# Attention blocks and MLP on one core: a list-scheduled instruction order, K halves by DMA, Q casts on GpSimd, and block 1's loads ahead of the weights

## The chip, the cores and the metric

One core of one Trainium2 chip. The metric is the device time of one execution in microseconds (us). The kernel before takes 338.56 us (median of three runs, 338.56 to 338.8). A profiled run also has a "span", from its first to its last instruction; it is about 2 us shorter than that run's device time. The profile of before was taken of a run of 340.03 us.

Engines in the profile: PE is TensorE's matmuls, PEld its weight loads, DVE is VectorE, ACT is ScalarE, POOL is GpSimd, SP is SyncE. A "q" behind the name (SPq, ACTq, POOLq) is the engine's sequencer issuing DMAs.

## The reference, cut to what matters

```python
batch, n_heads, seq, head_dim = (4, 8, 768, 64)        # q, k, v, float32
n_tokens, d_model, d_ff = (3072, 512, 2048)            # w_in, w_out, float32
def _attn_ref(q, k, v):                                # chunk = 32, top_k = 6
    ub = np.sum(np.maximum(q[..., None, :] * k_min, q[..., None, :] * k_max), axis=-1)  # bound per query and key chunk
    ...                                                # causal; the 6 chunks with the highest bound are kept
    scores = np.where(mask, scale * np.matmul(q, k.transpose(0, 1, 3, 2)), -1000000000.0)
    ...                                                # softmax
    return np.matmul(attn, v)
def _moe_ref(x, w_in, w_out):                          # x: the heads side by side, 3072 x 512
    h = x @ w_in
    g = np.where(h > 0.0, h, np.exp(np.minimum(h, 0.0)) - 1.0)
    return g @ w_out
```

## The kernel before

The work is cut into eight blocks: four batches, each in two halves of 384 queries. A block has four pairs of heads. Per pair there is a **front** (turn K and Q on TensorE, copy them, compute the bounds, select chunks), an **attention** part (scores, exp, mask, times V, normalize to `on`), and a transpose of `on` to `xt`: on TensorE in blocks 0 and 7, by a DMA on SyncE's queue in the others. When all four `xt` of a block are there, its **MLP** runs: 64 matmuls 128x384 into `h_ps` (called h below), exp, ELU to `gT`, 48 matmuls 128x512 into `o_ps` (called o), store. The next block's front and attention overlap with it.

The parts that the change touches (cuts are marked with `...`):

```python
def prep(t, hf):                                     # front of one pair
    ...
    for n in range(3):
        nc.tensor.transpose(ps[:, P * n:P * (n + 1)], k_pair[:, n], ident_f)   # psK
    ...                                              # VectorE: chunk minima and maxima, kmm and kst
    for h in range(2):                               # ScalarE: K of each head to lhs
        nc.scalar.activation(out=lhs[s][h][0:64, ts], in_=ps[64 * h:64 * h + 64, :], func=AF.Copy)
    ...                                              # psQ, the same way
    nc.scalar.activation(out=QTf[:, q0:HS], in_=ps[:, q0:HS], func=AF.Copy)
    for h in range(2):                               # ScalarE: Q of each head to rhs
        nc.scalar.activation(out=rhs[s][h][0:64, ts], in_=ps[64 * h:64 * h + 64, :], func=AF.Copy)
...
for t in pairs_of(0):
    load_v(t, 0)
front(0, span(-1, 0.0, 0.9))
casts = vpart(0)
w_ins = []
with tc.issue_after(casts[1].ins):                   # the weights, as soon as block 0's V is cast
    w_ins += [load_w_in(0), load_w_in(1)]
with tc.issue_after(casts[3].ins):
    w_ins += [load_w_in(2), load_w_in(3)]
    for i in range(4):
        load_w_out(i)
for i in range(len(blocks)):
    ...                                              # attend(...) x4, then mlp(...)
    if i + 1 < len(blocks):
        for d in load_block(i + 1):
            if i == 0:                               # block 1's loads wait for the whole w_in
                tc.add_manual_dep(d.ins, w_ins[GATE].ins.name, SYNC, reason="order")
        if i == 0:
            with tc.issue_after(mm_h[HGATE].ins):    # block 1's front after block 0's sixth h tile
                front(i + 1, at)
        ...
```

Each instruction has a priority from its stage (`span`, `at`), and the framework's scheduler orders each engine by it.

The softmax here doesn't subtract the row's maximum and nothing guards it: scores larger than these inputs give would overflow.

Of the kernel before, what the change touches and what calls it, by code (L numbers as in the profile page):

```python
# [9 lines left out]
AOT = mybir.AluOpType  # L10
# [5 lines left out]
B = 4  # L16
# [19 lines left out]
PE_T = (0, 7)  # L36
GATE = 3
HGATE = 5
SP_A = [(0.0, 0.5)] + [(0.0, 0.9)] * 7
SP_F = [(0.5, 1.0)] + [(0.0, 0.8)] * 7  # L40
SP_M = [(0.0, 1.0)] * 8
# [3 lines left out]
QHI = (HS, S)  # L45


@with_exitstack
def kernel(
# [9 lines left out]
    nc = tc.nc  # L59

    def pool(name, bufs, **kw):
        return ctx.enter_context(tc.tile_pool(name=name, bufs=bufs, **kw))

    const = pool("const", 1)
    ldpool = pool("ldpool", 4)
    qfpool = pool("qfpool", 3)
    smpool = pool("smpool", 4)
    selpool = pool("selpool", 3)
    ptpool = pool("ptpool", 9)
    opool = pool("opool", 3)  # L70
    xtpool = pool("xtpool", 12)
    gtpool = pool("gtpool", 2)
    mlppool = pool("mlppool", 4)
    psT = pool("psT", 1, space=bass.MemoryType.PSUM)
    psS = pool("psS", 2, space=bass.MemoryType.PSUM)
    psO = pool("psO", 1, space=bass.MemoryType.PSUM)
    psM = pool("psM", 4, space=bass.MemoryType.PSUM)

    warm = const.tile([P, 1], F32, name="warm")
    nc.vector.memset(warm, 0.0)  # L80
    nc.scalar.activation(out=warm, in_=warm, func=AF.Exp)
# [4 lines left out]
    def load_one(dst, x, t, hf, name, eng=nc.sync):  # L86
        b, r = divmod(t, NPAIR)
        xp = ldpool.tile([P, 3, 2, D], F32, name=name)
        dst[t, hf] = xp
        return [eng.dma_start(out=xp[:, :, h, :],  # L90
                              in_=x[b, 2 * r + h, HS * hf:HS * (hf + 1)].rearrange("(n p) d -> p n d", p=P))
                for h in range(2)]

    def load_qk(t, hf):
        first = t < 2 and hf == 0
        return (load_one(ldk, k, t, hf, "k_pair")
                + load_one(ldq, q, t, hf, "q_pair", nc.scalar if first else nc.sync))

    def load_v(t, hf):
        return load_one(ldv, v, t, hf, "v_pair")  # L100

    for t in range(NPAIR):
        load_qk(t, 0)


    ident_f = const.tile([P, P], F32, name="ident_f")
    nc.gpsimd.memset(ident_f, 0.0)
    nc.gpsimd.affine_select(out=ident_f, in_=ident_f, compare_op=AOT.not_equal,
                            fill=1.0, base=0, pattern=[[-1, P]], channel_multiplier=1)


    vexts, lhs, rhs, kst = [], [], [], []
    for s in range(NSET):
        vexts.append(const.tile([P, NQT, 2, D + 1], BF16, name=f"vext{s}"))
        lhs.append([const.tile([P, S], BF16, name=f"lhs{s}{h}") for h in range(2)])
        rhs.append([const.tile([P, S], BF16, name=f"rhs{s}{h}") for h in range(2)])
        kst.append(const.tile([P, 2, 2, CHUNK], F32, name=f"kst{s}"))

    eone = const.tile([P, NCH, 1], BF16, name="eone")
    nc.gpsimd.memset(eone, MASKNEG)  # L120
    nc.gpsimd.affine_select(out=eone[64:96], in_=eone[64:96],
                            compare_op=AOT.is_equal, fill=0.0, base=0,
                            pattern=[[1, NCH], [0, 1]], channel_multiplier=-1)
    econst = const.tile([P, NCH, CHUNK], BF16, name="econst")

    def init_set(s):
        for h in range(2):
            nc.vector.tensor_copy(out=lhs[s][h][64:96, :],
                                  in_=econst[64:96].rearrange("p c w -> p (c w)"))
            nc.gpsimd.memset(rhs[s][h][64:96, 0:Q0], 0.0)  # L130
        nc.gpsimd.memset(vexts[s][:, :, :, D:D + 1], 1.0)

    hsel = const.tile([P, 2], F32, name="hsel")
    for h in range(2):
        nc.gpsimd.memset(hsel[64 * h:64 * h + 64, h:h + 1], 1.0)
        nc.gpsimd.memset(hsel[64 * (1 - h):64 * (1 - h) + 64, h:h + 1], 0.0)
    for s in range(NSET):
        nc.gpsimd.memset(kst[s], 0.0)  # L138

    ident_b = const.tile([P, P], BF16, name="ident_b")  # L140
    nc.gpsimd.tensor_copy(out=ident_b, in_=ident_f)
    tri01 = const.tile([P, P], BF16, name="tri01")
    nc.gpsimd.memset(tri01, 1.0)
    nc.gpsimd.affine_select(out=tri01, in_=tri01, compare_op=AOT.is_ge,
                            fill=0.0, base=0, pattern=[[1, P]], channel_multiplier=-1)
    selb = []
    for hf in range(2):
        nb = (QHI[hf] - QLO[hf]) // CHUNK
        selb.append([const.tile([P, nb, CHUNK], BF16, name=f"selb{hf}{i}") for i in range(2)])
        for i in range(2):  # L150
            nc.gpsimd.memset(selb[hf][i], 0.0)

    w_in_sb = const.tile([P, NKK, DFF], BF16, name="w_in_sb")
    w_out_sb = const.tile([P, NFC, DMODEL], BF16, name="w_out_sb")
# [3 lines left out]
    def load_w_in(i):  # L158
        return nc.gpsimd.dma_start(out=w_in_sb[:, :, 512 * i:512 * (i + 1)], in_=wi[:, :, 512 * i:512 * (i + 1)])

    def load_w_out(i):
        nc.gpsimd.dma_start(out=w_out_sb[:, 4 * i:4 * i + 4, :], in_=wo[:, 4 * i:4 * i + 4, :])

    def cast_v(t, hf):
        return nc.gpsimd.tensor_scalar(out=vexts[t % NSET][:, 3 * hf:3 * hf + 3, :, 0:D], in0=ldv.pop((t, hf)),
                                       scalar1=1.0, scalar2=0.0, op0=AOT.mult, op1=AOT.add)
# [4 lines left out]
    def prep(t, hf):  # L171
        s = t % NSET
        ts = slice(HS * hf, HS * (hf + 1))
        k_pair, q_pair = ldk.pop((t, hf)), ldq.pop((t, hf))
        kmm = smpool.tile([P, 2, HCH], F32, name="kmm")
        pool0 = (psM, "psm") if (t < NPAIR and hf == 0) else (psT, "ps")
        ps = pool0[0].tile([P, HS], F32, name="psK", tag=pool0[1])
        for n in range(3):
            nc.tensor.transpose(ps[:, P * n:P * (n + 1)], k_pair[:, n], ident_f)  # L179
        pv = ps[:, :].rearrange("p (c w) -> p c w", w=CHUNK)  # L180
        nc.vector.tensor_reduce(out=kmm[:, 0, :], in_=pv, axis=AX.X, op=AOT.min)  # L181
        nc.vector.tensor_reduce(out=kmm[:, 1, :], in_=pv, axis=AX.X, op=AOT.max)  # L182
        for h in range(2):
            nc.scalar.activation(out=lhs[s][h][0:64, ts], in_=ps[64 * h:64 * h + 64, :], func=AF.Copy)  # L184
        cs = slice(HCH * hf, HCH * (hf + 1))
        nc.vector.tensor_tensor(out=kmm[:, 1, :], in0=kmm[:, 1, :], in1=kmm[:, 0, :], op=AOT.subtract)
        nc.vector.tensor_tensor(out=kst[s][:, :, :, cs],
                                in0=kmm[:, :, :].rearrange("p (w o) c -> p w o c", o=1)
                                .to_broadcast([P, 2, 2, HCH]),
                                in1=hsel[:, :].rearrange("p (o h u) -> p o h u", o=1, u=1)  # L190
                                .to_broadcast([P, 2, 2, HCH]), op=AOT.mult)
        q0 = QLO[hf] - HS * hf
        QTf = qfpool.tile([P, HS], F32, name="QTf")
        Qrl = qfpool.tile([P, HS], F32, name="Qrl")
        qf[t, hf] = (QTf, Qrl)
        ps = pool0[0].tile([P, HS], F32, name="psQ", tag=pool0[1])
        for n in range(3):
            nc.tensor.transpose(ps[:, P * n:P * (n + 1)], q_pair[:, n], ident_f)  # L198
        nc.scalar.activation(out=QTf[:, q0:HS], in_=ps[:, q0:HS], func=AF.Copy)  # L199
        for h in range(2):  # L200
            nc.scalar.activation(out=rhs[s][h][0:64, ts], in_=ps[64 * h:64 * h + 64, :], func=AF.Copy)
        nc.vector.tensor_scalar(out=Qrl[:, q0:HS], in0=QTf[:, q0:HS], scalar1=0.0, scalar2=None,  # L202
                                op0=AOT.max)


    def select(g, hf):
        qlo, qhi = QLO[hf], QHI[hf]
        nq = qhi - qlo
        nb = nq // CHUNK
        b0 = qlo // CHUNK  # L210
        ncs = qhi // CHUNK
        q0 = qlo - HS * hf
        pool0 = (psM, "psm") if (g < 2 and hf == 0) else (psT, "ps")
        ub = pool0[0].tile([P, HS], F32, name="ub", tag=pool0[1])
        for w in range(2):
# [8 lines left out]
        if b0 + 1 < 8:  # L224
            nc.vector.memset(ubT[:, 0, b0 + 1:8], -BIG)
        thr8 = selpool.tile([P, HCH, 8], F32, name="thr8")
        for i in range(nb):
            nc.vector.max(out=thr8[:, i, :], in_=ubT[:, i, 0:max(8, b0 + i + 1)])
# [222 lines left out]
```

## Time and profile before

| | before |
|---|---|
| device time, median of 3 | 338.56 us |
| span of the profiled run (of 340.03 us) | 338.3 us |
| TensorE / VectorE / ScalarE / GpSimd busy | 90 / 66 / 68 / 29 % |
| first h matmul / last o_sb copy | 32.6 / 335.4 us |

From the page of the kernel before: busy us with share of the span and number of instructions; then the busy tenths of TensorE in 40 slices of 8.5 us (PEclk is the granted TensorE clock in tenths); then the chain of waits that ended last, by engine.

```profile
span 338.3 us, 6875 instructions
PE 303.8 (90%) x2328; PEld 165.8 (49%) x2328; DVE 223.2 (66%) x690; ACT 231.4 (68%) x506; POOL 98.3 (29%) x219
...
PE   3776999998899979999989998999999998999895
...
PEclk9955799999999998999999999999999999999999
...
PE 32%; DVE 24%; issue 18%; ACT 17%; POOL 5%; DMA 3%; SPq 0%; POOLq 0%; ACTq 0%
```

TensorE looks full, and yet the chain that decides the time runs over TensorE for only 32% of the span. The page "Perfetto Trace Analysis" of the Trainium skill (section "Identifying the Most-Contended Engine") says that the matmul busy share is not a good measure of how close TensorE is to its peak.

So I use another measure throughout, worked out from the traces. At full clock the matmuls of one kind start 162 ns (h), 216 ns (o), 30 ns (times V) and 109 ns (fp32 transposes) after one another. Giving each matmul its own full-clock time of this kind, all 2,328 add up to 262.5 us of **matmul work** (an estimate: what one gives the small kinds that are not listed here shifts the sum and the waits below by up to 1.5 us, in all kernels alike). Where a matmul starts later than the one before it allows, that is TensorE's **wait**. Before, from the first matmul at 4.1 us: 36.5 us of waits for matmuls that start in the first 100 us, 32.4 us after that.

What TensorE waited for, from the view of waits (engine, line, tile, what released it: us in total, times, longest us). It lists only gaps that the trace can attribute. The 4.1 us of the second line are the wait from the span's start; the first K load landed at 4.0 us.

```profile
PE h_ps L321 <- DMA xt<-on: 4.6, 5, 2.3
PE psK L179 <- POOL kst_146 L138: 4.1, 1, 4.1
PE pxt L306 <- DVE on L299: 3.7, 3, 1.4
PE h_ps L321 <- DVE gT L328: 3.5, 8, 1.0
```

Busy time of each engine in four stretches (from:to in us, length, then busy us and number of instructions of each engine, mean granted clock, DMA share, GB/s):

```profile
0.00:32.00 32.00, 20.27 (x137) 12.34 (x137) 25.06 (x82) 16.58 (x34) 18.80 (x63) 0.77 0.99 181
32.00:60.00 28.00, 26.49 (x146) 13.61 (x147) 19.56 (x56) 17.63 (x39) 9.99 (x20) 0.90 0.87 180
60.00:100.00 40.00, 35.95 (x323) 19.73 (x321) 28.46 (x100) 36.25 (x80) 4.97 (x10) 1.00 0.40 98
100.00:320.00 220.00, 206.41 (x1653) 113.06 (x1652) 144.94 (x445) 155.37 (x343) 60.19 (x119) 0.99 0.30 76
```

Two things to read here. In the first 32 us VectorE (third count) is busy 25.06 us and ScalarE (fourth) 16.58 us. And after 100 us no engine but TensorE comes near its limit: ScalarE has 155 of 220 us. The DMA share (the time of the packets over that of 16 engines), on the other hand, is 0.99 in the first stretch and 0.87 in the second.

The operations that the change takes from ScalarE, from the list of groups (columns: line, engine, operation, tiles, shapes, count, busy us, mean ns). There are 32 such groups of four, two shown; per pair and half the kernel makes two `lhs` and two `rhs` copies of 0.49 us.

```profile
L184 ACT ACTIVATE lhs_143<-psK 64x384 bf16<-64x384 f32 x4 | 1.9, 487 | 0.0
L201 ACT ACTIVATE rhs_139<-psQ 64x384 bf16<-64x384 f32 x4 | 1.9, 487 | 0.0
```

The end of the start phase, from the timeline of TensorE (start us, duration, engine, line, operation, shapes, count, and in brackets the idle time before it):

```profile
32.27 0.50 PE L306 MATMUL pxt<-ident_b,on 128*128 128x128 bf16 x3 [1.36 <-DVE on L299]
32.56 6.50 PE L321 MATMUL h_ps<-xt,w_in_sb 128*128 128x384 bf16 x24
```

The first h waits for the last pair's `on` and not for the weights: `w_in` had landed by 26.5 us.

### The profile page before, as it was taken

To read this page: it belongs to the slowest core of one execution; us is meant where nothing else is said; L and a number is where in the kernel's file an instruction comes from. 1 tells how busy PE (TensorE), PEld (TensorE's weight loads), DVE (VectorE), ACT (ScalarE), POOL (GpSimd) and SP (SyncE) were. 2 spreads that over 40 slices of the span, in tenths; PEclk is the share of its full clock that TensorE was granted. 3 is DMA by queue.
4 is the path that set the end of the run, shared out by engine and by line. 5 is a ranking of instruction groups with operands and counts; after the bars stand their busy time and mean duration, and the time that the engine had idled before them with its cause. 6 is when DMAs were issued, how large, how long until landed. Compare 5 with 4: busy or idle time off the path is not lost.

```text
span 338.3 us, 6875 instructions
## 1 busy us (share of the span) xinstructions
PE 303.8 (90%) x2328; PEld 165.8 (49%) x2328; DVE 223.2 (66%) x690; ACT 231.4 (68%) x506; POOL 98.3 (29%) x219
## 2 busy tenths in 40 slices
PE   3776999998899979999989998999999998999895
PEld 2444544444454435555654455555554445545552
DVE  5888578566798673875479874866479765622640
ACT  5643585799995718976797649966797647856531
POOL 8750442000055214641153003420053004400530
PEclk9955799999999998999999999999999999999999
DMA  7899977542422677566232313223200111000001
GB/s 175 163 186 202 200 161 175 155 114 60 103 51 60 137 179 186 133 140 148 71 87 52 98 56 89 61 58 92 75 14 12 45 39 37 0 33 34 31 24 69
DMA packets 94498, 32.16 MB, mean 95 GB/s; under 512 B 87296, under 2 KB 91392, under 8 KB 94464
## 3 DMA queue, kind: packets, MB, share of 16 engines
q1 hardware_dynamic: 88640, 27.15, 32.8%
q0 software_dynamic: 4224, 4.19, 7.6%
q10 hardware_dynamic: 1600, 0.39, 0.5%
q8 instruction: 18, 0.29, 0.4%
q14 instruction: 16, 0.13, 0.1%
HBM read 27.26 MB, written 6.29 MB: 99 GB/s over the span
## 4 chain that ended last, share of the span: by engine, by line
PE 32%; DVE 24%; issue 18%; ACT 17%; POOL 5%; DMA 3%; SPq 0%; POOLq 0%; ACTq 0%
PE o_ps L334 11%; PE h_ps L321 9%; DVE gT L328 6%; ACT pt L265 5%; ACT e_sb L325 4%; PE sps L262 4%; PE ub L220 3%; POOL e_sb L326 3%; DMA xt<-on 2%; DVE kmm L181 2%; DVE kmm L182 2%; PE psK L179 1%; DVE on L299 1%; DVE ubT L223 1%; DMA v_pair<-in_v_dram 1%
## 5 line engine op out<-in xcount | busy, mean ns | idle before, releaser
L326 POOL TENSOR_SCALAR e_sb<-e_sb 128x384 f32<-128x384 f32 x128 | 65.7, 521 | 190.8 <-ACT e_sb L325 186.9
L321 PE MATMUL h_ps<-xt,w_in_sb 128*128 128x384 bf16 x512 | 107.1, 334 | 8.3 <-DMA xt<-on 4.6
L334 PE MATMUL o_ps<-w_out_sb,gT 128*128 128x512 bf16 x384 | 99.5, 379 | 0.9 <-DVE gT L328 0.8
L328 DVE SCALAR_TENSOR_TENSOR gT<-h_ps,e_sb 128x384 bf16<-128x384 f32 x128 | 69.1, 552 | 32.7 <-POOL e_sb L326 30.9
L265 ACT ACTIVATE pt<-sps 128x384 bf16<-128x384 f32 (+1 forms) x160 | 79.0, 538 | 16.6 <-PE sps L262 15.3
L325 ACT ACTIVATE e_sb<-h_ps 128x384 f32<-128x384 f32 x128 | 61.3, 502 | 30.5 <-PE h_ps L321 29.9
L321 PEld LDWEIGHTS <-w_in_sb 128*128 128x128 bf16 x512 | 49.6, 100 | 40.8 <-issue 17.2
L334 PEld LDWEIGHTS <-gT 128*128 128x128 bf16 x384 | 35.4, 97 | 36.5 <-issue 3.8
L337 ACT ACTIVATE o_sb<-o_ps 128x512 f32<-128x512 f32 x24 | 14.3, 598 | 35.4 <-PE o_ps L334 32.2
L293 PEld LDWEIGHTS <-pt 128*128 128x128 bf16 x672 | 29.2, 100 | 17.6 <-DVE pt L274 5.1
L274 DVE TENSOR_TENSOR pt<-pt,tri_196 128x512 bf16<-128x512 bf16 x32 | 14.3, 446 | 18.8 <-ACT pt L265 18.8
L179 PE MATMUL psK<-ident_f,k_pair 128*128 128x128 f32 x96 | 20.0, 300 | 6.1 <-POOL kst_146 L138 4.1
L181 DVE TENSOR_REDUCE kmm<-psK 128x12 f32<-128x384 f32 x32 | 17.6, 550 | 6.3 <-PE psK L179 6.1
L268 ACT ACTIVATE pt<-sps 128x512 bf16<-128x512 f32 x32 | 19.5, 609 | 2.6 <-PE sps L262 2.2
L199 ACT ACTIVATE QTf<-psQ 128x192 f32<-128x192 f32 (+1 forms) x32 | 13.2, 413 | 10.1 <-PE psQ L198 7.0
L198 PE MATMUL psQ<-ident_f,q_pair 128*128 128x128 f32 x96 | 18.3, 304 | 1.2 <-ACT lhs_155 L184 0.3
L202 DVE TENSOR_SCALAR Qrl<-QTf 128x192 f32<-128x192 f32 (+1 forms) x32 | 11.7, 365 | 11.5 <-ACT QTf L199 11.0
L179 PEld LDWEIGHTS psK<-ident_f,k_pair 128*128 128x128 f32 x96 | 12.0, 149 | 13.0 <-POOL kst_146 L138 4.1
L182 DVE TENSOR_REDUCE kmm<-psK 128x12 f32<-128x384 f32 x32 | 17.5, 547 | 0.0
L198 PEld LDWEIGHTS psQ<-ident_f,q_pair 128*128 128x128 f32 x96 | 11.3, 151 | 11.8 <-ACT lhs_155 L184 2.0
L280 DVE TENSOR_TENSOR pt<-pt,tri_196 128x256 bf16<-128x256 bf16 x32 | 10.6, 333 | 7.7 <-ACT pt L268 7.7
L223 DVE STREAM_TRANSPOSE ubT<-ub 128x192 f32<-128x192 f32 (+1 forms) x16 | 7.7, 480 | 11.3 <-PE ub L220 11.3
(348 smaller groups left out, 400.7 us busy)
## 6 DMA issues: line engine op xcount, KB each, us to landing
k_pair<-in_k_dram SPq DMA_DIRECT2D x64, 96.0 KB, 2.5
v_pair<-in_v_dram SPq DMA_DIRECT2D x64, 96.0 KB, 2.4
out_dram<-o_sb SPq DMA_DIRECT2D x24, 256.0 KB, 2.1
q_pair<-in_q_dram SPq DMA_DIRECT2D x60, 96.0 KB, 2.4
w_in_sb<-in_moe_w_in_dram POOLq DMA_DIRECT2D x4, 512.0 KB, 8.4
w_out_sb<-in_moe_w_out_dram POOLq DMA_DIRECT2D x4, 512.0 KB, 17.0
q_pair<-in_q_dram ACTq DMA_DIRECT2D x4, 96.0 KB, 2.9
xt<-on SPq DMA_TRANSPOSE x24, 2.4
```

Source lines behind the costliest of these rows:

```text
L179: nc.tensor.transpose(ps[:, P * n:P * (n + 1)], k_pair[:, n], ident_f)
L181: nc.vector.tensor_reduce(out=kmm[:, 0, :], in_=pv, axis=AX.X, op=AOT.min)
L182: nc.vector.tensor_reduce(out=kmm[:, 1, :], in_=pv, axis=AX.X, op=AOT.max)
L198: nc.tensor.transpose(ps[:, P * n:P * (n + 1)], q_pair[:, n], ident_f)
L265: nc.scalar.activation(out=pt[:, hd, 0:wtot], in_=sps[:, 0:wtot], func=AF.Exp, scale=SCALE)
L268: nc.scalar.activation(out=pt[:, :, 0:256], in_=sps[:, :].rearrange("p (h w) -> p h w", h=2), func=AF.Exp, scale=SCALE)
L293: nc.tensor.matmul(o3[:, hd, qi, :], lhsT=pt[:, hd, P * qt + off:P * qt + off + P], rhs=vexts[s][:, kb, hd, :], start=(kb == 0), stop=(kb ...
L321: mm = nc.tensor.matmul(hw, lhsT=w_in_sb[:, kk, P * fc:P * (fc + 1)], rhs=xT[NPAIR * b + kk, hf], start=(kk == 0), stop=(kk == NKK - 1))
L325: nc.scalar.activation(out=e_sb, in_=hw, func=AF.Exp)
L326: last_e = nc.gpsimd.tensor_scalar(out=e_sb, in0=e_sb, scalar1=-1.0, scalar2=1.0, op0=AOT.add, op1=AOT.mult)
L328: nc.vector.scalar_tensor_tensor(out=gT[:, fc, :], in0=hw, scalar=0.0, in1=e_sb, op0=AOT.max, op1=AOT.min)
L334: nc.tensor.matmul(o_ps, lhsT=gT[:, fc, P * tt:P * (tt + 1)], rhs=w_out_sb[:, fc, :], start=(fc == 0), stop=(fc == NFC - 1))
```

## The change

Its intent has four parts. (1) **Order**: the kernel no longer leaves the order to the framework. It states every operation with its engine, its duration and its latency, list-schedules them itself, and emits the instructions in that order. (2) **K and Q**: from block 2 on, K is cast once on ScalarE (`kb`) and its two halves moved to `lhs` by DMAs on SyncE's queue; Q's halves are cast by GpSimd from `QTf`. (3) **Start**: block 1's loads and front come before the weights' DMAs. (4) Fronts may run further ahead, as far as buffers allow. The arithmetic is the same.

```diff
 def prep(...):
-        for h in range(2):
-            nc.scalar.activation(out=lhs[s][h][0:64, ts], in_=ps[64 * h:64 * h + 64, :], func=AF.Copy)
+        if direct:                                   # i in DIRECT = (0, 1); as before
...
+        else:
+            kb = buf("kb", [P, HS], BF16)
+            op("ACT", 390, 140, lambda: nc.scalar.activation(out=kb.get(), in_=psk.get(), func=AF.Copy),
+               reads=[psk], writes=[kb])
+            for h in range(2):
+                op("SP", 490, (200, ), lambda h=h: nc.sync.dma_start(
+                    out=lhs[s][0:64, h, ts], in_=kb.get()[64 * h:64 * h + 64]), reads=[kb], writes=[r_lhs[s][hf]])
...
+            for h in range(2):
+                pool_op(480, lambda h=h: nc.gpsimd.tensor_scalar(
+                    out=rhs[hf][g][0:64, h, j, :], in0=qtf.get()[64 * h:64 * h + 64], scalar1=1.0, scalar2=0.0,
+                    op0=AOT.mult, op1=AOT.add), [r_q[hf][g][j]], [qtf])
...
+    def run(self):                                   # class Plan: greedy list schedule
...
+                    t = max(o.ready, free[e])        # earliest start: inputs, engine, a free buffer
+                    for x in o.bufs:
+                        if x not in held:
+                            t = max(t, min(slots[x.cls], default=1e18))
+                    if t < 1e17 and (best[e] is None or (t, o.prio, o.id) < best[e][:3]):
+                        best[e] = (t, o.prio, o.id, o)
...
+    loads(0)
+    front(0)
+    loads(1)
...
+    casts = front(1)
+    span(-0.2, 0.0, 0.1)
+    for i in range(4):
+        load_w_in(i, [casts[0]])                     # after block 1's first V cast
+    for i in range(4):
+        load_w_out(i, [casts[0]])
...
+    plan.run()
+    with tc.manual_schedule():
+        for o in plan.order:
+            o.fn()
```

The other lines of the diff mostly rewrite every `nc.engine.op(...)` as `op(engine, duration, latency, ...)`. Two things go with it: `rhs` and `selb` are laid out in other buffers, and the Q loads of the first two pairs are issued by SyncE instead of ScalarE.

## The prediction

> What bounds the kernel now. TensorE is busy 303.8 of 338.3 us (the page's first part), but busy is not work: back to back, the timeline's start-to-start times are 162 ns for a 128x384 matmul (h_ps), 216 ns for 128x512 (o_ps), 30 ns for 128x65, 109 ns for an fp32 transpose. Summed over all 2,328 matmuls (an estimate from those figures) that is about 262 us. The other 76 us are waits and half clock. By stretch of the timeline: first matmul at 4.1 us; before the first h_ps at 32.6 us about 19 us are lost; 2.5 us more until 40 us (granted clock 0.50 in 20 to 30 us, 0.63 in 30 to 40); about 14 us in 40 to 97; about 12 and 10 us in the two 76 us periods that follow; 8 us from 249 to 316; 4 us of tail. "TensorE: Matmul & The Clock Gate" of the Trainium skill (the HAM clock gate) says that a sparse TensorE is gated to half clock; the 0.50 agrees.
>
> The waits are short and many: TensorE waits for ScalarE (psT and sps not yet evacuated), for xt transposes and for gT. ScalarE is busy 57.7 and VectorE 53.1 of the 76 us from 173 to 249 (windows view); neither is full, so order and latency cost here, not throughput.
>
> What the change does.
> 1. ScalarE: in blocks 2 to 7 (24 pairs) it drops 96 copies 64x384 of 0.48 us (46 us), adds 24 K casts 128x384 of about 0.49 (12 us), widens 12 QTf (2 us). Net about -32 us summed; busy 231 to about 200.
> 2. GpSimd gets 48 Q casts of about 0.5 us (estimate from its 0.52 us V casts): busy 98 to about 120. The page "GPSIMD Engine Reference" (Specifications) says it shares SBUF interfaces with VectorE; with e_sb behind casts, 1 to 3 us in all.
> 3. SyncE gets 48 more DMA issues of about 0.5 us, landing in about 2 us, a block ahead of need: off the chain.
> 4. Start: block 1's loads go before the weights, which issue at 12 us now, at about 24 us then; the first h_ps comes at about 30 us, no later than today's 32.6, since that one waits for pxt, not weights. Meanwhile ScalarE, idle 45% of the first 32 us, works on block 1. ScalarE bounds this phase: fronts and attention of blocks 0 and 1 are about 45 us of it. Gain 7 to 9 us.
> 5. Order: a greedy list schedule with true durations, fronts two blocks ahead. With the lighter ScalarE I expect the four later stretches to go from 44 us of waits to about 27: gain about 17 us.
>
> Sum: 338.5 - 8 - 17 = 313 us. Range 304 to 326. Chances: faster 0.87, within 2% 0.09, slower 0.04.
>
> What would show it. Same matmul count and start-to-start times; ScalarE busy about 200, GpSimd about 120; the period of two blocks 76 to about 71 us; lhs and rhs copies gone as releasers of psK/psQ after block 1; at 55 us, where the first o_sb comes now, about 8 us more matmul work done; the end (last h_ps burst to last store) unchanged, about 25 us.
>
> What would make it wrong. The schedule's model has no half clock: if TensorE stays at half clock beyond 40 us, engines block behind a waiting instruction. Weights landing later than 35 us would leave TensorE idle. In-order SyncE (K halves, xt, loads in one queue) could hold xt. VectorE may become the next limit, above all if GpSimd's casts slow it. If the waits are latency that order cannot hide, the gain is only the start's: about 330.

## The result, and the profile after

| | before | after |
|---|---|---|
| device time, median (range, runs) | 338.68 us (338.56 to 339.42, 4) | 324.92 us (324.62 to 327.04, 4) |
| ratio | | 0.9603 (95%: 0.956 to 0.9646) |
| matmul work started by 60 / 100 us | 30.9 / 59.8 us | 25.5 / 59.8 us |
| waits of TensorE, first 100 us / after | 36.5 / 32.4 us | 35.5 / about 18 us |
| first h | 32.6 us | 44.2 us |
| end of block 1 / end of block 7 (last o copy) | 123.7 / 335.4 us | 126.0 / 320.0 us |

A ratio here is the mean time of one kernel's runs over that of the other's of the same rounds, so it is not quite the ratio of the medians. Executions over 1.5% slower than the fastest of the same kernel are left out of the means. The "about 18" is 21.9 us, less some 3.7 us for about 17 o matmuls whose records are missing from this trace (2,309 of 2,328 are there; each is 0.216 us of work that looks like a wait).

The result lies in the predicted range, 12 us above the predicted point. The split says more than the sum: from the end of block 1 to the end of block 7 the kernel now takes 194.0 us instead of 211.7, 17.7 us less. Up to the end of block 1 it takes 2.3 us more. (Up to 1.6 us of this split can belong to the two profiled runs.)

The same parts of the page after:

```profile
span 322.9 us, 6923 instructions
PE 291.1 (90%) x2309; PEld 167.5 (52%) x2328; DVE 226.1 (70%) x690; ACT 200.5 (62%) x434; POOL 123.3 (38%) x255
...
PE   4578699899997799999998999999998989999995
...
PEclk9975659999999999999999999999999999999999
...
PE 70%; DVE 13%; ACT 8%; issue 3%; DMA 2%; SPq 1%; POOL 1%; ACTq 0%; POOLq 0%
```

ScalarE and GpSimd moved as foreseen (231.4 to 200.5, 98.3 to 123.3 us). The chain that ended last now runs over TensorE for 70% of the span instead of 32%: more of the time is decided by TensorE's own stream, although its busy share is the same. The share does not follow the time closely, though: it is 44% in e2, which is no faster than before, and 76% in e10, which is 5 us slower than after. ("issue" is time for which the profile shows no wait; it fell from 18 to 3%.) The view of waits after:

```profile
PE psS L441 <- ACT pt L457: 6.8, 18, 0.8
PE psM L320 <- DMA kld<-in_k_dram: 4.0, 1, 4.0
PE psT L320 <- ACT lhs L340: 2.9, 2, 2.7
PE psM L320 <- ACT rhs L369: 2.9, 1, 2.9
PE psM L524 <- DVE gT L532: 2.8, 5, 0.8
```

The waits for `xt` and `pxt` that led before are gone from the head of the list. What is left is the exchange of scores and exp with ScalarE (18 waits, none over 0.8 us) and three long waits, all in the first 41 us (that of 4.0 us is again the one for the first load). The stretches after:

```profile
0.00:32.00 32.00, 19.70 (x121) 12.09 (x122) 27.97 (x86) 19.46 (x42) 17.25 (x53) 0.82 0.84 171
32.00:60.00 28.00, 23.63 (x176) 12.95 (x175) 19.63 (x67) 17.57 (x41) 6.73 (x13) 0.78 1.14 199
60.00:100.00 40.00, 37.62 (x340) 21.56 (x341) 29.43 (x94) 26.95 (x58) 18.57 (x37) 1.00 0.63 149
100.00:320.00 220.00, 210.12 (x1676) 120.87 (x1691) 149.07 (x446) 136.49 (x295) 80.75 (x154) 1.00 0.31 78
```

At the start VectorE is now busy 27.97 of 32 us, and the DMA share between 32 and 60 us is 1.14, against 0.87 before. The end of the start phase, on TensorE's timeline:

```profile
40.34 0.56 PE L320 MATMUL psT<-ident_f,qld 128*128 128x128 f32 x3 [2.67 <-ACT lhs L340]
...
42.95 0.51 PE L507 MATMUL psM<-ident_b,on 128*128 128x128 bf16 x3
43.25 0.84 PE L320 MATMUL psT<-ident_f,kld 128*128 128x128 f32 x3
43.89 0.52 PE L441 MATMUL psS<-rhs,lhs 96*128 96x384 bf16 x1
44.21 2.12 PE L524 MATMUL psM<-xt,w_in_sb 128*128 128x384 bf16 x6
```

The first h follows block 0's last `pxt` (42.95 us) within 1.3 us, as it did before. The weights are not what it waits for: the first quarter of `w_in` landed at 30.9 us, the last at 40.9. Transposes and scores of block 1 (lines 320 and 441) stand between block 0's last steps, and one of them, a Q transpose at 40.34 us, stopped TensorE for 2.67 us in front of everything behind it.

SyncE's queue during that time and later, from its timeline:

```profile
30.89 5.16 SPq L296 DMA_DIRECT2D vld<-in_v_dram  x2
36.15 4.71 SPq L296 DMA_DIRECT2D kld<-in_k_dram  x2
40.96 4.80 SPq L296 DMA_DIRECT2D qld<-in_q_dram  x2
...
64.99 1.83 SPq L348 DMA_DIRECT2D lhs<-kb  x2
66.91 1.29 SPq L512 DMA_TRANSPOSE xt<-on  x1
68.30 1.06 SPq L296 DMA_DIRECT2D qld<-in_q_dram  x2
69.46 2.03 SPq L296 DMA_DIRECT2D vld<-in_v_dram  x4
```

The durations are the time that SyncE needs to issue. A load costs about 0.5 us to issue at 69 us, but 2.4 us at 36 us, while the weights move (their last part landed at 54.3 us). The 13 issues from 25.8 us on took until 54.0 us; at 0.53 us each, as at 10 us, they would have needed 7 us, so some 21 us went there (an estimate from this trace; for 9 issues in the trace of before it is 8 us). Behind it there is no gap: in every 10 us of the first 120 us SyncE is issuing for 84 to 97% of the time. Before, it was 31 to 96% between 20 and 110 us, and it stood idle for all of 12 to 26 us.

### The profile page after: what moved, and what is told of

It reads as the page before. It is cut to its first block, busy times and chain, and to the rows that moved or that the text cites. A ratio compares the mean times of both kernels' runs of the same rounds, so it can differ in the third digit from the quotient of the medians.

```text
span 322.9 us, 6923 instructions
## 1 busy us (share of the span) xinstructions
PE 291.1 (90%) x2309; PEld 167.5 (52%) x2328; DVE 226.1 (70%) x690; ACT 200.5 (62%) x434; POOL 123.3 (38%) x255
## 3 DMA queue, kind: packets, MB, share of 16 engines
q0 software_dynamic: 4224, 4.19, 7.9%
## 4 chain that ended last, share of the span: by engine, by line
PE 70%; DVE 13%; ACT 8%; issue 3%; DMA 2%; SPq 1%; POOL 1%; ACTq 0%; POOLq 0%
PE psM L524 24%; PE psM L540 20%; PE psS L441 9%; PE psO L488 6%; PE psT L394 5%; PE psT L320 5%; ACT pt L457 4%; DVE lhs L283 2%; DVE kmm L335 2%; DMA vld<-in_v_dram 2%; DVE rhs L420 2%; SPq L296 1%; DVE thr L409 1%; ACT osb L544 1%; ACT QTf L365 1%
## 5 line engine op out<-in xcount | busy, mean ns | idle before, releaser
L524 PE MATMUL psM<-xt,w_in_sb 128*128 128x384 bf16 x512 | 99.8, 330 | 2.8 <-DVE gT L532 2.8
L530 POOL TENSOR_SCALAR e<-e 128x384 f32<-128x384 f32 x128 | 66.0, 520 | 85.3 <-ACT e L528 60.4
L540 PE MATMUL psM<-w_out_sb,gT 128*128 128x512 bf16 x365 | 93.1, 379 | 0.9 <-issue 0.3
L532 DVE SCALAR_TENSOR_TENSOR gT<-psM,e 128x384 bf16<-128x384 f32 x128 | 69.5, 552 | 25.4 <-POOL e L530 23.0
L457 ACT ACTIVATE pt<-psS 128x384 bf16<-128x384 f32 (+1 forms) x160 | 79.4, 539 | 11.6 <-PE psS L441 10.9
L528 ACT ACTIVATE e<-psM 128x384 f32<-128x384 f32 x128 | 63.0, 498 | 30.0 <-PE psM L524 28.9
L441 PE MATMUL psS<-rhs,lhs 96*128 96x384 bf16 (+2 forms) x288 | 64.5, 300 | 10.2 <-ACT pt L457 6.8
L540 PEld LDWEIGHTS <-gT 128*128 128x128 bf16 x384 | 35.9, 97 | 33.4 <-issue 2.4
L441 PEld LDWEIGHTS <-lhs 96*128 96x128 bf16 x288 | 26.7, 99 | 32.5 <-issue 12.5
L335 DVE TENSOR_REDUCE kmm<-psT 128x12 f32<-128x384 f32 x56 | 30.0, 547 | 4.5 <-PE psT L320 4.5
L488 PE MATMUL psO<-vext,pt 128*128 128x65 bf16 x672 | 31.1, 197 | 1.5 <-DVE pt L468 0.8
L420 DVE STREAM_TRANSPOSE rhs<-selb 32x192 bf16<-32x192 bf16 (+1 forms) x64 | 30.1, 470 | 1.4
L314 POOL TENSOR_SCALAR vext<-vld 128x384 bf16<-128x384 f32 x32 | 16.9, 535 | 35.3 <-DMA vld<-in_v_dram 28.9
L345 ACT ACTIVATE kb<-psT 128x384 bf16<-128x384 f32 x24 | 11.8, 494 | 25.8 <-issue 9.8
L461 ACT ACTIVATE pt<-psS 128x512 bf16<-128x512 f32 x32 | 19.5, 609 | 7.5 <-PE psS L441 7.4
L468 DVE TENSOR_TENSOR pt<-pt,tri 128x512 bf16<-128x512 bf16 x32 | 15.4, 480 | 10.9 <-ACT pt L457 10.3
```

The lines of the kernel that those rows point to most:

```text
L335: op("DVE", 475, 115, lambda w=w, o=o: nc.vector.tensor_reduce(out=kmm.get()[:, w, :], in_=psk.get()[:, :].rearrange("p (c w) -> p c w", w ...
L420: op("DVE", 585 if nq > 192 else 385, 50, lambda h=h, j=j, r0=r0: nc.vector.transpose(out=rhs[hf][g][64:96, h, j, q0:HS], in_=sb[r0:r0 + 3 ...
L441: nc.tensor.matmul(sps.get()[:, o + pc:o + pc + w], lhsT=lhs[s][0:96, hd, P * kb:P * (kb + 1)], rhs=rhs[hf][g][0:96, hd, j, cq:cq + w], st ...
L457: op("ACT", 390 if wtot <= 384 else 495, 130, lambda pt=pt, sps=sps, hd=hd, wtot=wtot: nc.scalar.activation(out=pt.get()[:, hd, 0:wtot], i ...
L488: nc.tensor.matmul(o3.get()[:, hd, qi, :], lhsT=pt.get()[:, hd, P * qt + off:P * qt + off + P], rhs=vexts[s][:, kb, hd, :], start=(kb == 0 ...
L524: op("PE", 161, 200, lambda fc=fc, kk=kk, h_ps=h_ps: nc.tensor.matmul(h_ps.get()[:, 0:HS], lhsT=w_in_sb[:, kk, P * fc:P * (fc + 1)], rhs=x ...
```

## The experiments

All kernels gave correct results, and all runs were fast but one of e9. Most of the variants that were meant to repair the start (e3 to e7, e9, e10) came out slower than the theory behind them had said. "Work" and "waits" are as defined above. A first pair of questions was what the gain is made of; a second, why the start gained nothing. For the start two theories stood at first: the weights come too late (e3), or block 1's front, which now goes first, gets in the way of block 0's end (e4). Later ones were VectorE (e5, e9) and the clock (e7, e10).

### e1: the order alone

```diff
-DIRECT = (0, 1)
+DIRECT = tuple(range(8))
```

The kernel after, with the old ScalarE copies of K and Q in all blocks.

> The list schedule with the old ScalarE copies in all eight blocks (no K halves by DMA, no Q casts on GpSimd). ScalarE busy should be back at about 231 us, GpSimd near 98. Theory 'order and latency bind, ScalarE's load is beside the point': about 326 us. Rival 'the lighter ScalarE makes the steady gain': about 334 to 338 us, the stretch from the last o_ps of block 1 to that of block 7 back near the 212 us of before (194 in the change).

Measured: 323.24 us (322.27 to 325.16), ratio to before 0.9538 (0.9497 to 0.9579). ScalarE is back at 228.1 us and GpSimd at 95.4; the waits after 100 us are 17.2 us. Its page:

```profile
PE 290.7 (91%) x2328; PEld 168.8 (53%) x2328; DVE 225.0 (70%) x690; ACT 228.1 (71%) x506; POOL 95.4 (30%) x207
...
PEclk9999969999999999999999999999999999999999
```

The change without its K and Q moves gives all of the gain; "order" here takes in the new start and the other buffers. ScalarE, 28 us busier than in the kernel after, cost nothing. It is also the fastest kernel, and the simpler one; by the scatter that e11 and e12 show below, its 1.7 us over the kernel after are no proof that it is better.

### e2: the offload alone

```diff
+        moved = t >= NPAIR                           # from block 2 on
+        if moved:
+            kb = kbpool.tile([P, HS], BF16, name="kb")
+            nc.scalar.activation(out=kb, in_=ps, func=AF.Copy)
...
+                nc.sync.dma_start(out=lhs[s][h][0:64, ts], in_=kb[64 * h:64 * h + 64])
...
+                nc.gpsimd.tensor_scalar(out=rhs[s][h][0:64, ts], in0=QTf[64 * h:64 * h + 64, :], scalar1=1.0,
+                                        scalar2=0.0, op0=AOT.mult, op1=AOT.add)
```

The kernel before, its order left to the framework, with the K halves and Q casts moved.

> The old order and old start, with K halves by DMA and Q cast by GpSimd from block 2 on. ScalarE busy about 200 us. Theory 'order binds': 335 to 339 us. Rival 'ScalarE's load binds': 325 to 330 us, the first 97 us unchanged and the gain all after it.

Measured: 339.55 us (339.06 to 341.62), ratio 1.0023 (0.9983 to 1.0063): the same. Its last stretch:

```profile
100.00:320.00 220.00, 204.75 (x1645) 113.99 (x1644) 146.61 (x440) 128.71 (x283) 80.54 (x157) 0.99 0.34 84
```

ScalarE fell from 155.37 to 128.71 us there and TensorE started no more matmuls for it (1,645 against 1,653). Waits after 100 us: 33.0 us, against 32.4. The four corners together, medians in us:

| | K, Q on ScalarE | K by DMA, Q on GpSimd |
|---|---|---|
| framework's order | 338.7 (before) | 339.6 (e2) |
| list-scheduled order, new start | 323.2 (e1) | 324.9 (after) |

### e3: weights earlier

```diff
-        load_w_in(i, [casts[0]])                     # block 1's first V cast
+        load_w_in(i, [casts0[1 if i < 2 else 3]])    # block 0's V casts, as before the change
...
-        load_w_out(i, [casts[0]])
+        load_w_out(i, [casts0[3]])
```

> The change with the weights issued after block 0's V casts again (about 12 us instead of 24). Theory A 'weights after block 1's loads cost the start': first h_ps at about 33 us instead of 44, total 5 to 8 us less than the change's 324.9. Rival B 'the fixed order runs block 1's front ahead of block 0's last pair, so xt is late': first h_ps stays at 42 to 45 us and the total within 2 us of 325; weights land by 31 us and wait.

Measured: 328.74 us (328.19 to 329.25), ratio 0.9692. `w_in` was complete at 33.5 us, the first h came at 39.4 us, 4.8 us earlier than in the kernel after. Yet block 1 ended at 128.1 us, 2.1 us later. The early weights did not remove the loss; that h still came 6 us after the weights agrees with what was read above, that it does not wait for them.

### e4: block 1's front planned behind block 0's attention

```diff
+    gate = []                                        # block 0's last attention matmuls
-        op("PE", 335, 200, lambda: transposes(psk, k_ld), reads=[k_ld, r_ident_f], writes=[psk])
+        op("PE", 335, 200, lambda: transposes(psk, k_ld), reads=[k_ld, r_ident_f], writes=[psk], after=gate)
...                                                   # the same for psq; applies to block 1 only
```

Block 0's attention is also entered into the plan before block 1's front; its priorities stay.

> The change with the K and Q transposes of block 1 (and so its whole front) held behind the last attention matmul of block 0, in the plan's order; loads and weights as in the change. Theory B: first h_ps at 31 to 34 us, matmul work done at 60 us 4 to 6 us more than the change's 25.5; total about 319 to 322. Theory A: first h_ps is held by the weights (first slice lands at 30.9), little gained: 324 to 326. Third view 'half clock binds the start whatever the order': first h_ps at 36 to 40.

Measured: 326.22 us (325.1 to 327.22), ratio 0.9619 (0.9578 to 0.966). The first h came at 33.5 us, 10.7 us earlier than after. So block 1's front was what held it: this is shown. But it did not pay. Against the kernel after, matmul work was 2.8 us ahead at 60 us and 3.0 ahead at 80 us, and 1.1 us behind at 100 us. Block 1's first h came at 90.6 us against 92.1. A gain of 3 us was there, and was gone 20 us later. The total lies above the 319 to 322 us that the theory had said.

### e5: the selector rows of lhs by DMA, from ScalarE's queue

```diff
-        for h in range(2):                           # VectorE, 16 copies 32x768
-            op("DVE", 390, 60, lambda h=h: nc.vector.tensor_copy(out=lhs[s][64:96, h, :], ...
+        op("ACT", 500, (200, ), lambda: nc.scalar.dma_start(out=lhs[s][64:96, :, :], ...
```

This takes VectorE's largest job of the first 20 us away.

> The change, with the 16 copies of the selector rows into lhs (8.4 us of VectorE in the first 26 us) replaced by 8 DMAs issued by ScalarE. Theory 'VectorE bounds the start, not ScalarE': first h_ps moves from 44 to about 36 to 38 us, matmul work at 60 us up by 4 to 6 us, total 319 to 322. Rival 'the start is bound elsewhere (half clock, psT, weights)': first h_ps within 2 us of 44, total within 1.5 us of 325.

Measured: 327.46 us (326.12 to 328.57), ratio 0.9645; first h at 41.0 us. It is confounded. The issue of the first four DMAs took ScalarE's queue 5.27 us, during the first pairs' copies:

```profile
6.51 5.27 ACTq L282 DMA_DIRECT2D lhs<-econst  x4
11.83 0.33 ACT L365 ACTIVATE QTf<-psM 128x192 f32<-128x192 f32 x1 [9.52 <-DMA kld<-in_k_dram]
```

The cost moved from one engine to another, and the plan had changed as well. e9 repeats the test with the order kept.

### e6: e1, e4 and e5 together

The edit is the three diffs above in one kernel, in the hope of a version that beats both.

> Old copies in all blocks (e1), block 1's front held behind block 0's attention (e4), selector rows by DMA (e5). If the three are independent, e1 gives -1.7 us and e5 what it gives alone: 316 to 320, first h_ps at about 29 to 31 us, bounded below by the first weights at 30 us. If the first 100 us are bound by something that none of them touches, 322 to 324.

Measured: 330.49 us (329.26 to 331.65), ratio 0.9747. A miss: 7 us slower than e1, with the first h at 35.2 us. But the early h did last here until the end of block 1, which came at 121.3 us, the earliest of all kernels; its `xt` transposes were issued 0.2 to 2.1 us after their input. What was lost came later: from the end of block 1 to that of block 7 e6 takes 202.8 us, e1 195.0. Why is not known.

### e7: a plan that knows of the half clock

The granted clock on the page is 0.5 to 0.7 in places before 40 us, and the plan's durations are those of full clock.

```diff
             o.start = t
+            o.occ *= 2 if o.eng == "PE" and t < 36000 else 1
```

> The change, its plan told that TensorE takes twice as long in the first 36 us (fp32 transposes stand 213 ns apart there, 109 later). Theory 'the plan is wrong at the start because it knows no half clock': first h_ps earlier by 4 us or more, total 319 to 322. Rival 'the plan's order is not what costs the start': total 323 to 327.

Measured: 329.17 us (327.28 to 330.71), ratio 0.9694; first h at 43.3 us. The truer durations of TensorE did not help.

### e8: a plan with flat durations

```diff
+        if eng in ("ACT", "DVE", "POOL"):
+            o.occ, o.lat = 400, (lat if isinstance(lat, tuple) else 150)
```

How much of the gain is owed to the durations, and how much to fixing an order by dependencies and buffers at all?

> The change, its plan told that every ScalarE, VectorE and GpSimd instruction takes 400 ns and shows 150 ns later (TensorE's and the DMAs' durations kept). Theory 'the gain comes from true durations': most of it is lost, 331 to 338. Rival 'issuing what is ready first is enough, roughly right durations do': 323 to 328.

Measured: 332.25 us (330.73 to 333.75), ratio 0.9787. The waits after 100 us are 20.5 us: most of what the order saves there (32.4 to about 18) does not need durations that tell operations apart. Work at 100 us is 56.0 us, 3.8 less than after. By the ends of blocks, 2.6 of the 7.6 us between the two traces were lost by the end of block 1 (128.6 us) and 5.0 after it (199.0 us to the end of block 7 instead of 194.0), so the durations mattered in both parts.

### e9: the selector rows by DMA from GpSimd's queue, the order kept

```diff
-            op("DVE", 390, 60, lambda h=h: nc.vector.tensor_copy(out=lhs[s][64:96, h, :],
-                                                                 in_=econst[64:96].rearrange("p c w -> p (c w)")),
+            op("DVE", 390, 60, lambda h=h: h or nc.gpsimd.dma_start(
+                out=lhs[s][64:96, :, :],
+                in_=econst[64:96].rearrange("p (o c) w -> p o (c w)", o=1).to_broadcast([32, 2, S])),
```

The plan is told the same durations, so every other instruction keeps its place; only VectorE's 16 copies become eight DMAs. These stand in GpSimd's queue in front of the weights, whose last part landed at 55.1 us instead of 54.3.

> The change in its own order, only that the 16 VectorE copies of the selector rows (8.4 us in the first 26 us) are 8 DMAs issued by GpSimd instead; nothing else is planned anew. In e5 ScalarE's queue stalled over its DMA issues from 6.5 to 11.8 us, which hid the answer. Theory 'VectorE bounds the start': VectorE busy in the first 32 us falls from 28.0 to about 19, first h_ps from 44 to 36 to 39 us, total 319 to 322. Rival 'something else bounds it': first h_ps 42 to 45 us, total 323 to 327.

Measured: 326.76 us (324.5 to 330.12; the last was slow, and the median of the three fast runs is 326.56), ratio 0.9629 (0.9575 to 0.9682). VectorE's busy time in the first 32 us fell to 20.41 us:

```profile
0.00:32.00 32.00, 22.41 (x146) 13.08 (x150) 20.41 (x74) 20.23 (x44) 20.60 (x61) 0.90 0.86 188
```

The first h came at 41.0 us, 3.2 us earlier than after. Matmul work was 3.2 us ahead at 60 us and 3.3 at 80 us: VectorE did hold up the start, by about that much. At 100 us it was 1.3 us behind, and from there the two kernels run alike until the end of block 5 (265.6 and 265.4 us). As in e4, the lead is lost between 80 and 100 us, and here the trace shows where it goes. TensorE's timeline, then SyncE's:

```profile
93.19 3.88 PE L525 MATMUL psM<-xt,w_in_sb 128*128 128x384 bf16 x13 [4.53 <-DMA xt<-on]
```

```profile
67.69 1.29 SPq L513 DMA_TRANSPOSE xt<-on  x1
...
74.49 1.86 SPq L513 DMA_TRANSPOSE xt<-on  x1
...
81.16 1.21 SPq L513 DMA_TRANSPOSE xt<-on  x1
...
89.58 1.88 SPq L513 DMA_TRANSPOSE xt<-on  x1
```

TensorE stood 4.53 us waiting for an `xt` transpose. The four transposes of block 1 were issued at 67.7, 74.5, 81.2 and 89.6 us. In the kernel after they were issued at 66.9, 73.7, 80.0 and 88.3 us. Yet their input `on` was finished at 58.6, 67.9, 71.7 and 80.5 us in e9, 3.7 us earlier each time than after (62.3, 71.6, 75.4, 84.2). Earlier work on the other engines did not move the transposes: SyncE issued without a gap in front of them, in the same order as after. That it came 0.8 to 1.3 us later than there fits the weights, which landed 0.8 us later; this is not shown further. The transposes came 6.6 to 9.4 us after their input in e9, 2.1 to 4.6 us in the kernel after, and at once (0.0 to 0.1 us) in the kernel before.

### e10: TensorE kept warm at the start

Idle fp32 matmuls of the identity, into buffers about to be overwritten, in the planned gaps of TensorE before 36 us; the order is the kernel after's.

```diff
+            if o.eng == "PE" and o.start < 36000:
+                gap, free = o.start - free, o.start + o.occ
+                ...                                  # x: the op's PSUM buffer, not yet in use
+                    for _ in range(max(0, int(gap // 200))):
+                        nc.tensor.matmul(ps[:, 0:P], lhsT=ident_f, rhs=ident_f, start=True, stop=True)
```

> The change in its own order, with idle fp32 128x128 matmuls put into the gaps that the plan sees on TensorE before 36 us, written to the tile that the next real matmul overwrites. It should keep the clock up: fp32 transposes 109 ns apart instead of 213 by about 8 us. Theory 'half clock costs the start': first h_ps from 44 to 38 to 40 us, total 319 to 322. Rival 'TensorE's speed is off the path there': first h_ps 43 to 46 us, total 324 to 327. If the idle matmuls do not lift the clock it says nothing.

Measured: 330.29 us (327.4 to 331.88), ratio 0.9746. The transposes did run at 109 ns between 4 and 12 us and mostly between 16 and 30 us, where in the kernel after most stand 213 ns apart. But the 172 idle matmuls were 18.7 us of work (at 109 ns each) before 51 us, a stretch that has not that much room, and the first h came at 51.8 us. What the half clock costs is not settled by this.

### e11 and e12: the plan's durations 10% up, 10% down

```diff
+        if eng in ("ACT", "DVE", "POOL"):
+            o.occ = 1.1 * occ                        # e12: 0.9
```

These measure how much the time moves when only the order is drawn anew.

> The change, its plan told that ScalarE, VectorE and GpSimd take 10 per cent longer: no better and no worse a model, but another order. It measures how far any re-planning moves the time by chance. If the order is robust: 323.5 to 326.5. If the e3, e5 and e7 results (327 to 329) were chance of the new order: 322 to 330, anywhere.

> The same with 10 per cent shorter. With e11 it gives the spread of re-planned orders. Robust: 323.5 to 326.5. Chance: 322 to 330.

Measured: 327.05 us (324.32 to 328.09), ratio 0.9636, and 327.99 us (326.86 to 328.18), ratio 0.968. So plans that differ in nothing of substance lie up to 3 us apart, and the kernel after is the best of the three. This is the yardstick for all re-planned kernels: e4 and e5 (326 to 327 us) can't be told from it by their total, and e3 and e7 (about 329 us) hardly from e12; what is said of them rests on when things happened in their traces. e1, the fastest, is 1.7 us below the kernel after, and that is within it too.

## Why the prediction was right or wrong

The total lies in the range, 1.1 us below its upper end. Of the two gains in the sum one came and the other did not; it is the width of the range that covered this, not the sum. In that the total was lucky.

**Right: the order's gain in the steady part.** Point 5 expected 17 us less waiting in the later stretches. From the end of block 1 to the end of block 7 it was 17.7 us less, and the period of two blocks went from 75 to 78 us to about 70 us (71 was said). The mechanism is the one named, short waits that order and latency cause: waits after 100 us fell from 32.4 to about 18 us, h's alone from 11.4 to 4.6. It is no chance of one plan: the same stretch takes 193.2 to 197.0 us in all list-scheduled kernels but e6 (202.8) and e8 (199.0), and 212.8 us in e2. That 17.7 meets 17 so closely owes something to where the line is drawn. Point 5's stretches began at 40 us, and counted from 55 us, where point 4 was to be read, the gain is 4.1 + 15.4 = 19.5 us.

**Right: the moved operations.** ScalarE 200.5 us (about 200 was said), GpSimd 123.3 us (about 120). The end, from the first h of block 7 to the last o copy, went from 23.0 to 21.7 us (unchanged was said).

**Wrong in its reason: "With the lighter ScalarE".** Point 5 gave the order and the lighter ScalarE together 17 us. The four corners give the list-scheduled order all of it and the lighter ScalarE nothing: +0.9 us in the old order, +1.7 in the new one, the second within the scatter of re-planning. That follows from the prediction's own remark that ScalarE was not full; the point should have gone on to say that then its load buys nothing.

**Also misread: "fronts two blocks ahead".** The diff issues `front(i + 2)` in the loop, but a front's priority is still that of the block before its own, as before; only its loads have that of two blocks before. In the traces block 2's front (its K and Q transposes) runs from 54 to 76 us, during block 1's attention, and before from 65 to 87 us, during it too.

**Wrong: point 4, "Start ... Gain 7 to 9 us".** This is the step that failed, and it is 10 of the 12 us. The term was −8 us; by the end of block 1 it measured +2.3 us. At 55 us, where about 8 us more matmul work was expected, 4.1 us less was done (22.6 against 26.7 us). Three claims behind it fell:

- *"The first h_ps comes at about 30 us, no later than today's".* It came at 44.2 us. That it waits for pxt and not for weights was right, before and after. What was missed is that the work which fills the idle time then stands in front of pxt: block 1's front runs on the same in-order engines as block 0's last pair. e4 takes it out of the way and the first h comes at 33.5 us.
- *"ScalarE bounds this phase".* It had 16.58 of 32 us before; VectorE had 25.06, and 27.97 after. e9 frees VectorE and gains 3.2 us by 60 us. The number was in the profile of before; the prediction looked at the engine that would be idle less and not at the one that was busiest.
- *"off the chain"*, of SyncE in point 3. In e9 SyncE undid the repair. After the change SyncE issues without a gap until 120 us, and in e9 the xt transposes of block 1 are issued 0.8 to 1.3 us later than after, although their input is ready 3.7 us earlier. What e9 won at the start is given back there. "In-order SyncE could hold xt" stood among the things that could make the prediction wrong, and it was one; it should have been a term of the sum. That the K halves have their part in it is likely, not shown: e1 and e6, which do without them, are the only list-scheduled kernels whose block 1 ended earlier (122.6 and 121.3 us) than before the change (123.7).

The estimate that would have caught it uses the trace of before: 192 or so load issues of 0.5 us, 24 transposes of 1.2 us, 24 stores and the 48 new moves, with the loads of blocks 0 to 2 (72 issues) now all pressed into the first stretch, and each pair of issues taking 3 to 4 us while the weights move (4.23 us for two at 29.1 us in the trace of before).

**What stays open.** Only e1 and e6, which drop the K halves, relieved SyncE. None turned block 1's xt on TensorE or loaded V through another queue, so how much the start would then gain is not known. e1 is the nearest: without the K halves its first transposes wait 0 to 1.8 us instead of 2.1 to 4.6, and it has done 61.8 us of work by 100 us instead of 59.8, but it is re-planned too. A rival is left as well: between 32 and 60 us the DMA engines' share is 1.14, and it may be they, not SyncE's issuing, that hold its queue there; another queue would then not help. No run tells the two apart. e4's loss between 80 and 100 us is not plainly that of e9: its `on` of block 1 were finished at 61.6, 72.6, 80.4 and 83.8 us, the second and third later than after by 1 and 5 us, and its xt landed 6.1 us after their input on average, as they do after (6.2); only the last took longer (9.6 instead of 6.5 us). The cause is open there. The half clock's cost at the start is open too.

## What to carry to other kernels

Fill an idle stretch only after asking what the filler stands in front of on each in-order engine, and count the DMA-issuing queue as one of them: a queue that issues without a gap pins everything behind it, and takes back what is won elsewhere. When a change bundles a new order with lighter engines, run the corners apart; here an engine that was not full gave nothing back when it got lighter. With a generated schedule, perturb the generator's inputs first and learn the scatter (3 us here), before reading any single variant's total.

## What the Trainium skill lacked or had wrong

- "DMA: Bandwidth & Descriptors" (Issuing engines are not separate DMA queues) says that issuing from several engines saves only the sequencer's time to initiate a DMA, "which is usually small relative to the DMA itself". Here it is not small: 0.5 us per load of 96 KB that lands in about 2.5 us, 1.2 us per transpose, and together (the slow issues of the next point included) they fill SyncE to 84 to 97% for 120 us. "Perfetto Trace Analysis" (What "DMA-bound" means) does name this case, an issuing engine whose track is solid DMA slices, and the trace agrees.
- No page that I found gives the issue time while another queue moves large weights: about 0.5 us per load alone, 2.4 us each (4.71 us for two) at 36 us while GpSimd's 4.19 MB of weights moved. Nor the 5.27 us that four small DMAs between SBUF tiles held ScalarE's queue (e5).
- "TensorE: Matmul & The Clock Gate" (Part 1: The HAM clock gate) warns that clock events in the profile can be unreliable, and this agrees: in e1 the granted clock reads 0.9 or more in the first slices (its trace has no record of the clock before 35.9 us), and yet three fp32 transposes take 0.87 us at 3.83 us (213 ns apart, twice the 109 ns of later). Where there are records, they fit: in the kernel after the granted clock is 1.0 from 16.9 to 20.3 us, 0.5 to 37.3, 1.0 to 40.7 and 0.5 to 47.6 us, and its transposes stand 109 ns apart at 16 to 20 us and 213 ns apart at 24 to 30 us.
- "GPSIMD Engine Reference" (1. Specifications) says that GpSimd's SBUF interfaces are shared with VectorE, without saying how much that can cost a VectorE copy. The same copy of 32x768 took 0.35 us at 11.43 us, with GpSimd idle, as much at 10.17 us beside one of GpSimd's V casts, and 2.06 us among GpSimd's memsets (7.16 to 9.0 us). That the memsets were the cause is read from the times alone; from VectorE's timeline of the kernel after:

```profile
7.13 2.06 DVE L283 COPY lhs<-econst 32x768 bf16<-32x768 bf16 x1
...
10.17 0.35 DVE L283 COPY lhs<-econst 32x768 bf16<-32x768 bf16 x1
...
11.43 0.35 DVE L283 COPY lhs<-econst 32x768 bf16<-32x768 bf16 x1
```
